# Bucketed attention and two mixtures of experts on one core: buckets as twelve bit columns with their sums in the scores' tiles, and the integer tile of the weights' words in PSUM

## The chip, the core and the metric

One core of a Trainium2 chip runs the whole program in one launch. The metric is the device time of one execution in microseconds. The engines are TensorE (PE, with its weight loads as PEld), VectorE (DVE), ScalarE (ACT), GpSimd (POOL) and SyncE (SP), which issues nearly all DMAs. TensorE's clock has two levels, 1.2 and 2.4 GHz; the profile gives the granted clock of a stretch as a share of the higher one.

## What is computed

The reference, cut to the part that the change touches:

```
def _attn_ref(q, k, v, proj):             # q, k, v: 2 x 8 x 768 x 64, proj: 64 x 6
    q_bits = (np.einsum('bhsd,dk->bhsk', q, proj) > 0)
    k_bits = (np.einsum('bhsd,dk->bhsk', k, proj) > 0)
    q_bucket = np.sum(q_bits * powers, axis=-1)       # powers = 2 ** arange(6)
    k_bucket = np.sum(k_bits * powers, axis=-1)
    mask = q_bucket[:, :, :, None] == k_bucket[:, :, None, :]
    scores = np.where(mask, scale * np.matmul(q, k.transpose(0, 1, 3, 2)), -1000000000.0)
    scores = scores - np.max(scores, axis=-1, keepdims=True)
    attn = np.exp(scores)
    attn = attn / (np.sum(attn, axis=-1, keepdims=True) + 1e-09)
    return np.matmul(attn, v)
def _moe_ref(x, w_in, w_out):             # 1536 x 512, 512 x 2048, 2048 x 512
    h = x @ w_in
    return (h * (1.0 / (1.0 + np.exp(-1.702 * h)))) @ w_out
```

A query sees only the keys whose six sign bits are the same as its own. A dense layer follows (its two weight matrices arrive as 64-bit floats), and then a layer of eight experts with a noisy top-2 choice, which the change doesn't touch.

## The kernel before

**Tiling.** Attention is cut into 96 steps g: for each of 2 batches, 3 chunks of 256 queries, 4 pairs of heads, 2 heads and 2 halves of 128 queries, one score tile of 128 queries by 768 keys. A score is a sum of two products of 128 rows each (`qk`, line 256): one over the high and low parts of q and k, one over their high parts in 64 rows and the bucket in another 64. Numbers are kept to nearly fp32 by splitting each into two f16 parts, so that a product is three f16 products.

**A unit of q or k.** There are 24 units of q (two heads, 256 queries) and 16 of k (one head, 768 keys). `stack_hi` and `stack_lo` split the rows into tiles sa and sb (qsa, qsb, or ks), on VectorE, GpSimd (line 147, the residual) and ScalarE, and a DMA transposes sa. `buckets` multiplies the transposed rows by proj on TensorE, into a PSUM tile pb of which there is one; ScalarE copies it to pc (line 186). `one_hot` then compares (line 191), multiplies by powers of two (193), sums (196) and compares the bucket with the numbers 0 to 63 (202 or 205), which gives 64 one-hot columns; `stack_end` scales them on ScalarE in 28 of the 40 units (212) and a DMA transposes sb (213). A pair of one-hot rows adds nothing to the score where the buckets agree and takes a large number away where they don't.

**A step.** `rowmax` (line 268) is a custom VectorE op that reads the score tile from PSUM, negates it into tile e and keeps the smallest of -score/8 as a column mx; `expo` (277) takes exponentials on ScalarE with mx as bias; splits, transposes by DMA (`et<-er`) and the product with v follow. Score tiles are two, 128 x 1024 fp32 each, of which 768 columns are used.

**The weights of the dense layer** come in 32 blocks of 128 x 512 words. `w_bits` makes a 32-bit float of a 64-bit one with three integer ops on VectorE (lines 430, 433, 436) through a tile wf in SBUF, of which there is one; `w_split` makes the two f16 parts on ScalarE and GpSimd. All 32 blocks are spread over the steps up to g = 24.

**The order.** Functions are hung on steps by tables in `PARAM` (KA, QA, W, PV and others), and a scheduler that plans with its own durations sets the order on each engine up to step 100; after that the order is the program's. Engines run their lists in order. The dense layer of a chunk runs between the score products of the next one, and the experts follow the attention.

Of the kernel before, what the change touches and what calls it, by code (L numbers as in the profile page):

```python
# [36 lines left out]
NBITS = 6  # L37
NB = 2 ** NBITS
BIG = 65504.0
TOP = 3.0e38  # L40
# [18 lines left out]


@with_exitstack
def fused(ctx: ExitStack, tc: tile.TileContext, q, k, v, proj, w_in, w_out, w_gate, w_noise, noise,
# [13 lines left out]

    iota_i = consts.tile([128, NB], F16)
    nc.gpsimd.iota(iota_i, pattern=[[1, NB]], base=0, channel_multiplier=0,
                   allow_small_or_imprecise_dtypes=True)
# [52 lines left out]
    def stack_hi(nm, b, u):  # L132
# [9 lines left out]
        rows[nm, b, u] = sa, sb  # L142
        h0 = 0 if nm == "q" else 64
# [3 lines left out]
        nc.gpsimd.tensor_tensor(x.rearrange(FL), x.rearrange(FL), hi, op=OP.subtract)  # L147
# [40 lines left out]
    def one_hot(nm, b, u):  # L188
        pc = bks.pop((nm, b, u))
        nb, bb = pc.shape[1], pc[:, :, :NBITS]  # L190
        nc.vector.tensor_tensor(bb, bb, pc[:, :, NBITS:], op=OP.is_gt)
        yield
        nc.vector.tensor_tensor(bb, bb, pow2[:, None, :].to_broadcast([128, nb, NBITS]), op=OP.mult)
        yield
        bk = att.tile([128, nb], F32, name="bk", bufs=2)
        nc.vector.tensor_reduce(bk, bb, axis=AX.X, op=OP.add)
        yield
        oh = rows[nm, b, u][0][:, :, :, 64:].rearrange(FL)
        if PARAM["OE"](nm, b) != "D":
            eng = nc.gpsimd if PARAM["OE"](nm, b) == "P" else nc.vector  # L200
            for i in range(nb):
                eng.tensor_scalar(oh[:, i], iota_i, bk[:, i:i + 1], -BIG if nm == "k" else BIG,
                                        op0=OP.not_equal if nm == "k" else OP.is_equal, op1=OP.mult)
            return
        nc.vector.tensor_tensor(oh, iota_i[:, None, :].to_broadcast([128, nb, NB]),
                                bk[:, :, None].to_broadcast([128, nb, NB]), op=OP.is_equal)

    def stack_end(nm, b, u):
        sb, xt = rows.pop((nm, b, u))
        oh = sb[:, :, :, 64:].rearrange(FL)  # L210
        if PARAM["OE"](nm, b) == "D":
            nc.scalar.activation(oh, oh, AF.Identity, scale=BIG, bias=-BIG if nm == "k" else 0.0)
        nc.sync.dma_start_transpose(xt[:, 1].rearrange("p h c t -> p (h c) t"), sb.rearrange("p h c d -> p (h c d)"))
# [21 lines left out]
    def v_lo(b, u):  # L235
# [3 lines left out]
        nc.gpsimd.tensor_tensor(vt[:, :, 1, sl], x, vt[:, :, 0, sl], op=OP.subtract)  # L239
# [9 lines left out]
    def qk(g):  # L249
# [12 lines left out]
    def rowmax(g):  # L262
# [5 lines left out]
        nc.vector.tensor_tensor_reduce(e32, st[g]["ps"][:, :S], zero.to_broadcast([128, S]), -0.125, TOP,  # L268
                                       op0=OP.add, op1=OP.min, accum_out=mx[:, 1:2])

    def expo(g):
# [5 lines left out]
        nc.scalar.activation(e32, e32, AF.Exp, scale=-1.0, bias=st[g]["mx"][:, 1:2],  # L277
# [110 lines left out]
    def pv_out(b, cc, hp):  # L388
# [11 lines left out]
        nc.gpsimd.tensor_tensor(xt[:, hp, 1, :], xn, xt[:, hp, 0, :], op=OP.subtract)  # L400
# [830 lines left out]
```

## Time and profile before

| | |
|---|---|
| runs, us | 813.56, 815.48, 811.27 (median 813.56) |
| profiled execution, us | 812.06, of which the span is 810.4 |
| granted clock of TensorE, mean | 0.963 |
| busy: PE, DVE, ACT, POOL | 703.6, 539.5, 446.6, 271.1 us |
| instructions: PE, DVE, ACT, POOL | 5408, 1368, 866, 305 |

The table is read for a first picture only: TensorE is busy 87% of the span, VectorE 67%, but an average over the run mixes stages with different limits, so the rows below are cut by stretches of time. A group of instructions is named by its line of the program, the engine, the operation and the tiles that it writes and reads (`out<-in`). "Idle before" is the time in which the engine waited ahead of these instructions, with what ended most of the waiting.

### The profile page before, as it was taken

The page shows a single profiled execution, that of the slowest core. Times are in us where ns is not written, and L with a number is a line of the kernel's source. Part 1 is how long each engine was busy: PE and PEld are TensorE (multiplying, and loading weights), DVE is VectorE, ACT ScalarE, POOL GpSimd, SP SyncE. Part 2 cuts the span into 40 slices and gives each one's busy share as a digit, 9 for nine tenths or more (in the row PEclk, how much of TensorE's full clock was granted, in tenths as well). Part 3 has the DMA queues.
Part 4 walks back from the last instruction along what each step waited for, and adds up shares of the span by engine and source line. Part 5 has one row for each costly group of instructions (what it writes and reads, how often), then busy time and mean ns, then how long its engine had stood idle before and what let it go on. Part 6 is the DMA issues. An engine that isn't in the chain of part 4 may idle for free.

```text
span 810.4 us, 14910 instructions
## 1 busy us (share of the span) xinstructions
PE 703.6 (87%) x5408; PEld 435.3 (54%) x5409; DVE 539.5 (67%) x1368; ACT 446.6 (55%) x866; POOL 271.1 (33%) x305
## 2 busy tenths in 40 slices
PE   1576578988888898789899999998999999999995
PEld 1343346646754585458457667465555545555452
DVE  8998689997896879659878815682735436354220
ACT  3678768775775686467657614452634425344220
POOL 6444646651444045314212223331130211302113
PEclk9889779999999998999999999999999999999998
DMA  8999678999999898996798772837968577584213
GB/s 220 213 258 224 161 181 192 243 289 237 172 164 196 157 196 178 213 187 105 124 175 132 115 253 38 203 150 192 259 133 252 123 194 232 77 255 89 26 18 44
DMA packets 266943, 139.20 MB, mean 172 GB/s; under 512 B 224177, under 2 KB 242673, under 8 KB 266865
## 3 DMA queue, kind: packets, MB, share of 16 engines
q1 hardware_dynamic: 260848, 125.04, 68.6%
q0 software_dynamic: 6016, 13.16, 9.1%
q8 instruction: 43, 0.70, 0.4%
q14 instruction: 36, 0.29, 0.1%
HBM read 61.48 MB, written 23.20 MB: 105 GB/s over the span
## 4 chain that ended last, share of the span: by engine, by line
PE 41%; DVE 5%; DMA 4%; ACT 2%; issue 1%; POOL 1%; POOLq 0%; ACTq 0%; DVEq 0%
PE ph L837 15%; PE py L868 14%; PE px L473 6%; PE h L462 3%; DMA et<-er 2%; PE py L862 1%; PE pv L370 1%; PE s L256 1%; DVE th L492 1%; DVE er L325 1%; DMA xg<-slots 1%; DMA slots<-xr,si 0%; ACT er L316 0%; ACT gt L506 0%; DMA qt<-qsb 0%
## 5 line engine op out<-in xcount | busy, mean ns | idle before, releaser
L462 PE MATMUL h<-xt,wi 128*128 128x256 f16 x1152 | 142.2, 279 | 6.5 <-DVE th L492 3.2
L837 PE MATMUL ph<-xg,ew 128*128 128x400 f16 (+2 forms) x864 | 133.9, 317 | 4.3 <-DMA xg<-slots 3.7
L473 PE MATMUL px<-wo,gt 128*128 128x512 f16 x576 | 131.1, 379 | 0.1
L777 DVE SCALAR_TENSOR_TENSOR ew<-w,ew 128x1024 f16<-128x1024 f32 x64 | 77.8, 1226 | 78.6 <-ACT ew L776 78.6
L462 PEld LDWEIGHTS <-wi 128*128 128x128 f16 x1152 | 113.8, 100 | 29.5 <-issue 9.4
L868 PE MATMUL py<-ew,ht 128*128 128x512 f16 x576 | 125.8, 379 | 0.0
L885 POOL DMA_INDIRECT out_dram<-yo,ti x32 | 53.8, 1683 | 203.5 <-ACT yo L878 197.7
L256 PE MATMUL s<-kt,qt 128*128 128x512 f16 (+1 forms) x384 | 87.2, 350 | 37.0 <-DVE mx L268 31.3
L837 PEld LDWEIGHTS <-ew 128*128 128x128 f16 x864 | 81.9, 99 | 54.2 <-issue 6.2
L277 ACT ACTIVATE e<-e,mx 128x768 f32<-128x768 f32 x96 | 89.4, 931 | 29.3 <-DVE mx L268 23.4
L507 POOL TENSOR_TENSOR gt<-th,gt 128x512 f16<-128x512 f32 x48 | 60.7, 1266 | 123.9 <-ACT gt L506 123.5
L268 DVE CUSTOM_DVE_ANT_0 e<-s,zero 128x768 f32<-128x768 f32 x96 | 90.7, 949 | 7.0 <-PE pt L295 2.9
L868 PEld LDWEIGHTS <-ht 128*128 128x128 f16 x576 | 56.2, 98 | 67.0
L325 DVE SCALAR_TENSOR_TENSOR er<-e,mx,er 128x768 f16<-128x768 f32 x68 | 71.1, 1049 | 27.4 <-ACT er L316 26.8
L473 PEld LDWEIGHTS <-gt 128*128 128x128 f16 x576 | 54.9, 98 | 62.3 <-issue 0.6
L316 ACT ACTIVATE er<-e,mx 128x768 f16<-128x768 f32 x68 | 63.2, 930 | 41.8 <-DMA et<-er 27.5
L256 PEld LDWEIGHTS <-qt 128*128 128x128 f16 x384 | 36.6, 102 | 66.4 <-issue 41.0
L878 ACT ACTIVATE yo<-py,wv 128x512 f32<-128x512 f32 x24 | 16.5, 688 | 94.1 <-PE py L868 57.4
L847 ACT ACTIVATE ht<-ph 128x400 f16<-128x400 f32 (+2 forms) x72 | 33.5, 466 | 62.0 <-PE ph L837 61.3
L776 ACT ACTIVATE ew<-w 128x1024 f16<-128x1024 f32 x64 | 66.2, 1048 | 0.1
L848 DVE SCALAR_TENSOR_TENSOR ht<-ph,ht 128x400 f16<-128x400 f32 (+2 forms) x72 | 37.5, 524 | 39.3 <-ACT ht L847 39.1
L370 PE MATMUL pv<-et,vt 128*64 128x256 f16 x720 | 50.5, 281 | 9.3 <-DMA et<-er 9.3
(234 smaller groups left out, 942.5 us busy)
## 6 DMA issues: line engine op xcount, KB each, us to landing
w<-in_moe_w_dram SPq DMA_DIRECT2D x64, 512.0 KB, 5.8
wraw<-in_moe_w_in_dram SPq DMA_DIRECT2D x16, 512.0 KB, 4.6
wraw<-in_moe_w_out_dram SPq DMA_DIRECT2D x16, 512.0 KB, 4.3
slots<-blank SPq DMA_DIRECT2D x6, 1032.0 KB, 6.4
v<-in_v_dram SPq DMA_DIRECT2D x24, 192.0 KB, 4.5
out_dram<-zeros SPq DMA_DIRECT2D x13, 256.0 KB, 3.3
k<-in_k_dram SPq DMA_DIRECT2D x16, 192.0 KB, 3.9
q<-in_q_dram SPq DMA_DIRECT2D x24, 128.0 KB, 3.3
```

What stands on the lines that cost most here:

```text
L256: nc.tensor.matmul(ps[:, n0 * 128:n1 * 128], qt[:, s, h, t, :], kt[:, s, h, n0:n1, :].rearrange("p c t -> p (c t)"), start=(s == 0), stop= ...
L268: nc.vector.tensor_tensor_reduce(e32, st[g]["ps"][:, :S], zero.to_broadcast([128, S]), -0.125, TOP, op0=OP.add, op1=OP.min, accum_out=mx[: ...
L277: nc.scalar.activation(e32, e32, AF.Exp, scale=-1.0, bias=st[g]["mx"][:, 1:2], accum_out=sms[b, cc, hp][:, 2 * h + t:2 * h + t + 1] if g < ...
L316: nc.scalar.activation(er[:, 0], st[g]["e"], AF.Copy, scale=r)
L325: nc.vector.scalar_tensor_tensor(er[:, 1], d["e"], d["mx"][:, 3:4], er[:, 0], op0=OP.mult, op1=OP.subtract)
L462: nc.tensor.matmul(ph[:, a, :], wi[ws][:, d, f0:f0 + 128], xt[:, d, xs, :], start=(d == 0 and ws == 0 and xs == 0), stop=(d == HP - 1 and ...
L473: nc.tensor.matmul(px, gts[ci, f // 2][:, gs, f % 2, t * 128:t * 128 + 128], wo[ws][:, f, :], start=(f == 0 and gs == 0 and ws == 0), stop ...
L507: nc.gpsimd.tensor_tensor(gt[:, 1], th, gt[:, 0], op=OP.subtract)
L776: nc.scalar.activation(hi, x, AF.Copy, scale=SW1 if j == 0 else SW2)
L777: nc.vector.scalar_tensor_tensor(lo, x, SW1 if j == 0 else SW2, hi, op0=OP.mult, op1=OP.subtract)
L837: nc.tensor.matmul(ph[:, :c1 - c0], w[:, ws, d * FE + f * 128:d * FE + f * 128 + 128], xg[e, p][:, xs * HP + d, :], start=(d == 0 and ws = ...
L868: nc.tensor.matmul(py, ht[:, f, hs, t * 128:t * 128 + 128], w[:, ws, f * DM:(f + 1) * DM], start=(i == 0), stop=(i == n - 1))
```

## The change

A bucket becomes twelve columns in place of 64: six that hold a scaled 1 where the bit is set, and six where it isn't (for k the other way round), so that their product takes a large number away for each bit that differs. VectorE makes them with two comparisons; the remaining columns of sb are set to zero by a GpSimd memset for each unit (line 138 of the changed program). The bucket sums go to unused columns of the score tile that is two steps ahead, and no longer to pb. The second score product reads 76 rows. The row maximum is a plain tensor_scalar that keeps the largest score and leaves the sign, and a ScalarE op of one column makes the bias of the exponential. The integer tile of `w_bits` lies in PSUM, in the buffer that pb had. The flags XS, GS, XN and the lower-case letters of WS choose what the kernel did already; `w_rest` only drops a name.

```diff
+KB = 64 + 2 * NBITS
+FAR = 2.0 ** 31
...
+        nc.gpsimd.memset(sb[:, :, :, KB:].rearrange(FL), 0.0)
...
-        pb = psr.tile([128, nh * n, 2 * NBITS], F32, name="pb", bufs=1)
+        w0 = nh * n * 2 * NBITS
+        s = st.get(now[0] + 2)
+        if s is None:
+            s = {"ps": pss.tile([128, 1024], F32, name="s")}
+        a0 = s.get("end", S)
+        s["end"] = a0 + w0
+        assert s["end"] <= 1024
+        pb = s["ps"][:, a0:a0 + w0].rearrange("p (m k) -> p m k", k=2 * NBITS)
...
-        nb, bb = pc.shape[1], pc[:, :, :NBITS]
-        nc.vector.tensor_tensor(bb, bb, pc[:, :, NBITS:], op=OP.is_gt)
-        yield
-        nc.vector.tensor_tensor(bb, bb, pow2[:, None, :].to_broadcast([128, nb, NBITS]), op=OP.mult)
-        yield
-        bk = att.tile([128, nb], F32, name="bk", bufs=2)
-        nc.vector.tensor_reduce(bk, bb, axis=AX.X, op=OP.add)
-        yield
-        oh = rows[nm, b, u][0][:, :, :, 64:].rearrange(FL)
-        if PARAM["OE"](nm, b) != "D":
-            eng = nc.gpsimd if PARAM["OE"](nm, b) == "P" else nc.vector
-            for i in range(nb):
-                eng.tensor_scalar(oh[:, i], iota_i, bk[:, i:i + 1], -BIG if nm == "k" else BIG,
-                                        op0=OP.not_equal if nm == "k" else OP.is_equal, op1=OP.mult)
-            return
-        nc.vector.tensor_tensor(oh, iota_i[:, None, :].to_broadcast([128, nb, NB]),
-                                bk[:, :, None].to_broadcast([128, nb, NB]), op=OP.is_equal)
+        oh = rows[nm, b, u][0][:, :, :, 64:64 + 2 * NBITS].rearrange(FL)
+        for j in range(2):
+            nc.vector.tensor_tensor(oh[:, :, j * NBITS:(j + 1) * NBITS], pc[:, :, :NBITS], pc[:, :, NBITS:],
+                                    op=OP.is_le if j == (nm == "q") else OP.is_gt)
+            yield
...
-        oh = sb[:, :, :, 64:].rearrange(FL)
-        if PARAM["OE"](nm, b) == "D":
-            nc.scalar.activation(oh, oh, AF.Identity, scale=BIG, bias=-BIG if nm == "k" else 0.0)
+        oh = sb[:, :, :, 64:64 + 2 * NBITS].rearrange(FL)
+        nc.scalar.activation(oh, oh, AF.Copy, scale=-BIG if nm == "k" else BIG)
...
+            kr = KB if s else 128
             for n0, n1 in ((0, 4), (4, 6)):
-                nc.tensor.matmul(ps[:, n0 * 128:n1 * 128], qt[:, s, h, t, :],
-                                 kt[:, s, h, n0:n1, :].rearrange("p c t -> p (c t)"),
+                nc.tensor.matmul(ps[:, n0 * 128:n1 * 128], qt[:kr, s, h, t, :],
+                                 kt[:kr, s, h, n0:n1, :].rearrange("p c t -> p (c t)"),
                                  start=(s == 0), stop=(s == 1))
...
-        nc.vector.tensor_tensor_reduce(e32, st[g]["ps"][:, :S], zero.to_broadcast([128, S]), -0.125, TOP,
-                                       op0=OP.add, op1=OP.min, accum_out=mx[:, 1:2])
+        nc.vector.tensor_scalar(e32, st[g]["ps"][:, :S], -FAR, -TOP, op0=OP.max, op1=OP.max, accum_out=mx[:, 0:1])
...
-        nc.scalar.activation(e32, e32, AF.Exp, scale=-1.0, bias=st[g]["mx"][:, 1:2],
+        nc.scalar.activation(st[g]["mx"][:, 1:2], st[g]["mx"][:, 0:1], AF.Copy, scale=-0.125)
+        nc.scalar.activation(e32, e32, AF.Exp, scale=0.125, bias=st[g]["mx"][:, 1:2],
...
-            f = moe.tile([128, 512], F32, name="wf", bufs=1)
-            fi = f.bitcast(I32)
+            fi = psr.tile([128, 512], I32, name="pfi", tag="pb", bufs=1)
```

The scheduler plans anew, so the order moves on all engines, though by the step g hardly any. Three places:

VectorE at the first two score tiles. L191, L193, L196 and L205 are the bucket code of a unit, L268 the row maximum and the read of its accumulator, L430 the first op on the words. Before:

```order
L191 TENSOR_TENSOR pc<-pc 128x6x6
L268 ISA e_351,mx<-s,zero 128x768
L268 ISA mx 128x1
L268 ISA e_395,mx<-s,zero 128x768
L268 ISA mx 128x1
L193 TENSOR_TENSOR pc<-pc,pow_92 128x6x6
L191 TENSOR_TENSOR pc<-pc 128x4x6
L196 TENSOR_REDUCE bk<-pc 128x6
L193 TENSOR_TENSOR pc<-pc,pow_92 128x4x6
L430 TENSOR_SCALAR wf<-wraw 128x512
L205 TENSOR_TENSOR ks<-iota_i,bk 128x6x64
L196 TENSOR_REDUCE bk<-pc 128x4
```

After, where L196 is a comparison, L261 the row maximum and L423, L426 and L429 the ops on the words:

```order
L196 TENSOR_TENSOR ks<-pc 128x6x6 x2
L261 TENSOR_SCALAR e_332,mx<-s 128x768
L196 TENSOR_TENSOR ks<-pc 128x6x6 x2
L261 TENSOR_SCALAR e_374,mx<-s 128x768
L423 TENSOR_SCALAR pfi<-wraw 128x512
L426 SCALAR_TENSOR_TENSOR pfi<-wraw,pfi 128x512
L429 SCALAR_TENSOR_TENSOR wraw<-wraw,pfi 128x512
L196 TENSOR_TENSOR qsb<-pc 128x4x6 x2
```

A unit's four rows have become one row of two ops, which stands ahead of the row maximum in place of around it.

GpSimd at the start, ahead of the first residual of k (L147). Before:

```order
L528 IOTA tok 128x12
L532 MEMSET blank 128x8
L535 MEMSET blank_120 128x8
L718 MEMSET spacer 1x1
L518 AFFINE_SELECT before<-before 128x128
L533 IOTA blank 128x1
L537 IOTA blank_120 32x1 x4
L718 MEMSET spacer 1x1
L147 TENSOR_TENSOR k_136<-k_136,ks 128x384
```

After, where L144 is that residual and L138 the new memset:

```order
L540 MEMSET blank_109 128x8
L138 MEMSET ks 128x6x52
L138 MEMSET qsb 128x4x52
L138 MEMSET ks 128x6x52 x3
L138 MEMSET qsb 128x4x52
L723 MEMSET spacer 1x1
L538 IOTA blank 128x1
L542 IOTA blank_109 32x1 x4
L144 TENSOR_TENSOR k_125<-k_125,ks 128x384
```

Six memsets now stand ahead of the first residual.

TensorE where a unit of k has its bucket products (L181 and L182) near a score tile (L256). Before:

```order
L181 LDWEIGHTS kt
L181 MATMUL pb<-pk,kt 128x12
L256 LDWEIGHTS qt
L256 MATMUL s<-kt,qt 128x512
L256 LDWEIGHTS qt
L256 MATMUL s<-kt,qt 128x256
L256 LDWEIGHTS qt
L256 MATMUL s<-kt,qt 128x512
L256 LDWEIGHTS qt
L256 MATMUL s<-kt,qt 128x256
L182 LDWEIGHTS kt
L182 MATMUL pb<-pk,kt 128x6
```

After (L185 and L186, and L249):

```order
L249 LDWEIGHTS qt
L249 MATMUL s<-kt,qt 128x512
L249 LDWEIGHTS qt
L249 MATMUL s<-kt,qt 128x256
L249 LDWEIGHTS qt
L249 MATMUL s<-kt,qt 128x512
L249 LDWEIGHTS qt
L249 MATMUL s<-kt,qt 128x256
L185 LDWEIGHTS kt
L185 MATMUL s<-pk,kt 128x12
L186 LDWEIGHTS kt
L186 MATMUL s<-pk,kt 128x6
```

The bucket products stood wherever the scheduler had room, and now follow the score products of their tile and write the same tile s.

## Rows read from the trace of the kernel before

**Rows 1.** Stretches, busy us (xcount): PE, PEld, DVE, ACT, POOL; PEclk, DMA share, GB/s

```profile
0.00:160.00 160.00, 101.99 (x820) 68.02 (x822) 142.82 (x320) 113.28 (x248) 88.35 (x119) 0.88 0.90 209
160.00:240.00 80.00, 68.60 (x593) 45.27 (x592) 71.74 (x186) 56.26 (x117) 33.03 (x31) 1.00 1.05 224
240.00:440.00 200.00, 179.34 (x1516) 118.73 (x1516) 152.99 (x445) 128.30 (x258) 62.56 (x59) 0.97 0.92 166
440.00:812.00 372.00, 353.63 (x2487) 203.29 (x2482) 171.91 (x420) 148.78 (x247) 87.15 (x98) 0.99 0.60 147
```

**Rows 2.** Waits of TensorE, 0 to 160 us: total us, times, longest

```profile
PE s L256 <- DVE mx L268: 20.4, 12, 3.6
PE pb L181 <- DMA kt<-ks: 14.6, 3, 9.0
PE pb L181 <- DMA qt<-qsa: 7.4, 3, 3.7
```

**Rows 3.** Waits of VectorE, 0 to 160 us

```profile
DVE wf L430 <- DMA wraw<-in_moe_w_out_dram: 3.3, 2, 2.5
```

**Rows 4.** Waits of TensorE, 160 to 440 us

```profile
PE s L256 <- DVE mx L268: 10.9, 12, 1.8
PE pv L370 <- DMA et<-er: 9.3, 6, 2.9
...
PE pb L181 <- DMA qt<-qsa: 1.6, 1, 1.6
```

**Rows 5.** Busy us by stretch on tile pc: PE, DVE, ACT; PEclk, DMA, GB/s

```profile
0.00:160.00 160.00, 0.00 (x0) 14.68 (x51) 3.60 (x17) 0.88 0.90 209
160.00:240.00 80.00, 0.00 (x0) 6.40 (x21) 1.42 (x7) 1.00 1.05 224
240.00:440.00 200.00, 0.00 (x0) 12.21 (x48) 3.25 (x16) 0.97 0.92 166
```

**Rows 6.** Busy us by stretch on tile iota_i: DVE, POOL; PEclk, DMA, GB/s

```profile
0.00:160.00 160.00, 11.54 (x17) 0.19 (x1) 0.88 0.90 209
160.00:240.00 80.00, 5.10 (x11) 0.00 (x0) 1.00 1.05 224
240.00:440.00 200.00, 17.57 (x49) 0.00 (x0) 0.97 0.92 166
```

**Rows 7.** Groups by shape, VectorE: busy us, mean ns; idle before

```profile
L191 DVE TENSOR_TENSOR pc<-pc 128x24 f32<-128x24 f32 x24 | 7.3, 305 | 0.2 <-ACT pc L186 0.2
```

**Rows 8.** Busy us by stretch on tile wf: DVE; PEclk, DMA, GB/s

```profile
0.00:160.00 160.00, 61.64 (x85) 0.88 0.90 209
160.00:240.00 80.00, 9.25 (x12) 1.00 1.05 224
```

**Rows 9.** Instructions on tile wf: ns min/median/max, first and last start us

```profile
L430 DVE TENSOR_SCALAR wf<-wraw x32: 411/421/1400, 7.3 to 176.8; 128x512 int32<-128x512 int32 x32
L433 DVE SCALAR_TENSOR_TENSOR wf<-wraw,wf x32: 677/692/2151, 7.7 to 178.1; 128x512 int32<-128x512 int32 x32
```

**Rows 10.** Line 492, same columns

```profile
L492 DVE SCALAR_TENSOR_TENSOR th<-th,h x48: 652/680/690, 124.5 to 505.0; 128x512 f32<-128x512 f32 x48
```

**Rows 11.** Groups by shape, VectorE, the row maximum

```profile
L268 DVE CUSTOM_DVE_ANT_0 e<-s,zero 128x768 f32<-128x768 f32 x96 | 90.7, 949 | 7.0 <-PE pt L295 2.9 <-PE s L256 2.2
```

**Rows 12.** Groups by shape, VectorE, line 848 (reads PSUM)

```profile
L848 DVE SCALAR_TENSOR_TENSOR ht<-ph,ht 128x400 f16<-128x400 f32 x56 | 32.0, 571 | 30.3 <-ACT ht L847 30.2
...
L848 DVE SCALAR_TENSOR_TENSOR ht<-ph,ht 128x256 f16<-128x256 f32 x8 | 3.3, 417 | 0.5 <-ACT ht L847 0.5
```

**Rows 13.** Groups by shape, ScalarE

```profile
L683 ACT ACTIVATE d<-d 128x2 f32<-128x2 f32 x5 | 1.0, 194 | 3.5 <-DVE d L680 3.5
```

**Rows 14.** Timeline of GpSimd from the start: start us, us

```profile
1.10 0.20 POOL L81 MEMSET ident<- 128x128 f16 x1
...
1.66 0.09 POOL L90 MEMSET pow<- 128x1 f32 x1
...
3.88 0.92 POOL L147 TENSOR_TENSOR k<-k,ks 128x384 f32<-128x384 f32 x1 [0.42 <-DVE ks L146]
```

More of the change, by code (lines that the diff above doesn't have):

```diff
@@ L37 @@
 NBITS = 6
-NB = 2 ** NBITS
 BIG = 65504.0
+KB = 64 + 2 * NBITS
+FAR = 2.0 ** 31
 TOP = 3.0e38
@@ L75, in fused @@
     pss = pss_ctx.enter_context(tc.tile_pool(name="pss", bufs=2, space=bass.MemoryType.PSUM))
-    iota_i = consts.tile([128, NB], F16)
-    nc.gpsimd.iota(iota_i, pattern=[[1, NB]], base=0, channel_multiplier=0,
-                   allow_small_or_imprecise_dtypes=True)
     ident = consts.tile([128, 128], F16)
@@ L83, in fused @@
                             channel_multiplier=1)
-    zero = consts.tile([128, 1], F32)
-    nc.vector.memset(zero, 0.0)
     ident32 = consts.tile([128, 128], F32)
     nc.vector.tensor_copy(ident32, ident)
-    pow2 = consts.tile([128, NBITS], F32)
-    for i in range(NBITS):
-        nc.gpsimd.memset(pow2[:, i:i + 1], float(2 ** i))
     pr = {nm: consts.tile([128, 3, NBITS], F16, name=f"p{nm}") for nm in "qk"}
@@ L146, in stack_hi @@
         eng.tensor_scalar(hi, x.rearrange(FL), GX, GX, op0=OP.add, op1=OP.subtract)
-        nc.gpsimd.tensor_tensor(x.rearrange(FL), x.rearrange(FL), hi, op=OP.subtract)
+        eng = nc.gpsimd if PARAM["XS"](nm, b) == "P" else nc.vector
+        eng.tensor_tensor(x.rearrange(FL), x.rearrange(FL), hi, op=OP.subtract)
         yield
@@ L238, in v_lo @@
         sl = slice(h * 64, h * 64 + 64)
-        nc.gpsimd.tensor_tensor(vt[:, :, 1, sl], x, vt[:, :, 0, sl], op=OP.subtract)
+        eng = nc.gpsimd if PARAM["XS"]("v", b) == "P" else nc.vector
+        eng.tensor_tensor(vt[:, :, 1, sl], x, vt[:, :, 0, sl], op=OP.subtract)
     st, ets, xts, pos, sms = {}, {}, {}, {}, {}
@@ L399, in pv_out @@
         nc.scalar.activation(xt[:, hp, 0, :], xn, AF.Copy)
-        nc.gpsimd.tensor_tensor(xt[:, hp, 1, :], xn, xt[:, hp, 0, :], op=OP.subtract)
+        eng = nc.gpsimd if PARAM["XN"] == "P" else nc.vector
+        eng.tensor_tensor(xt[:, hp, 1, :], xn, xt[:, hp, 0, :], op=OP.subtract)
     wi = [wts.tile([128, HP, FF], F16, name=f"wi{i}", tag="w") for i in range(2)]
@@ L441, in w_split, with w_rest @@
         hi, lo, src, scale = wblocks[i]
-        f = wraw.pop(i)
-        if PARAM["WS"](i) == "P":
-            nc.gpsimd.tensor_scalar(f, f, scale, 1.0, op0=OP.mult, op1=OP.mult)
-        else:
-            nc.scalar.activation(f, f, AF.Copy, scale=scale)
-        nc.scalar.activation(hi, f, AF.Copy)
-        nc.gpsimd.tensor_tensor(lo, f, hi, op=OP.subtract)
+        f, m = wraw[i], PARAM["WS"](i)
+        if m == "P":
+            nc.gpsimd.tensor_scalar(hi, f, scale, 1.0, op0=OP.mult, op1=OP.mult)
+        elif m == "A":
+            nc.scalar.activation(hi, f, AF.Copy, scale=scale)
+        else:
+            if m == "p":
+                nc.gpsimd.tensor_scalar(f, f, scale, 1.0, op0=OP.mult, op1=OP.mult)
+            else:
+                nc.scalar.activation(f, f, AF.Copy, scale=scale)
+            nc.scalar.activation(hi, f, AF.Copy)
+            nc.gpsimd.tensor_tensor(lo, f, hi, op=OP.subtract)
+    def w_rest(i):
+        hi, lo, src, scale = wblocks[i]
+        f = wraw.pop(i)
+        if PARAM["WS"](i) in "AP":
+            nc.vector.scalar_tensor_tensor(lo, f, scale, hi, op0=OP.mult, op1=OP.subtract)
     gts, mst = {}, {}
@@ L506, in moe_split @@
             nc.scalar.activation(gt[:, 0], th, AF.Copy)
-            nc.gpsimd.tensor_tensor(gt[:, 1], th, gt[:, 0], op=OP.subtract)
+            eng = nc.gpsimd if PARAM["GS"](ci, i) == "P" else nc.vector
+            eng.tensor_tensor(gt[:, 1], th, gt[:, 0], op=OP.subtract)
             if (ci, i) in clear:
@@ L972, in fused @@
                 soon(g + 1, w_split, wl)
+                at(g + 1, w_rest, wl)
                 wl += 1
@@ L1027, in fused @@
     g_lo = min(todo)
+    now = [0]
     for g in range(g_lo, G1 + 1):
+        now[0] = g
         if g == max(PARAM["GM"], g_lo):
```

1 line of the change is left out of this document (added).

## Prediction

> **What bounds the kernel now.** I read the stretches of the whole run first [rows 1]. From 440 us on, TensorE is busy 353.6 of the last 370 us and VectorE 171.9: next to nothing that the change touches lies there, so whatever it saves or costs before 440 us arrives at the end one for one. Before that the kernel has three different limits. In 0 to 160 us VectorE is busy 142.8 of 160 us, TensorE 102.0, ScalarE 113.3, GpSimd 88.4. In 160 to 240 us VectorE (71.7 of 80) and TensorE (68.6) are both near full and the DMA share is 1.05. In 240 to 440 us TensorE leads with 179.3 of 200, VectorE has fallen to 153.0.
>
> Then the waits. In 0 to 160 us TensorE's largest wait is for the row maxima that set a score tile free (20.4 us); after it come the transposes of k, of whose 14.6 us 9.0 are the very first load, and those of q with 7.4 [rows 2]. VectorE's own longest wait there is 3.3 us in all [rows 3]: it is the engine that others wait for. In 160 to 440 us TensorE still waits 10.9 us for row maxima, and 9.3 for the transposes of the exponentials [rows 4]. So a VectorE microsecond is worth most of a microsecond before 160 us, perhaps half until 240, and little after.
>
> **The bucket code on VectorE.** Before, a unit (24 of q, 16 of k) costs a comparison, a product and a sum on tile pc, and then the one-hot columns from iota_i. By stretch, pc and iota_i together take 14.7 + 11.5 = 26.2 us, 6.4 + 5.1 = 11.5 us and 12.2 + 17.6 = 29.8 us [rows 5, 6]. ScalarE's copies into pc count the units: 17, 7 and 16 [rows 5]. After, a unit is two comparisons like line 191, of 0.305 us on average [rows 7]: 34 x 0.305 = 10.4, 14 x 0.305 = 4.3 and 32 x 0.305 = 9.8 us, so -15.8, -7.2 and -20.0 us. The output is now f16 in rows 128 columns apart, a form that no row of this op has. I bound one comparison by half and by twice that mean, 0.15 and 0.6: 12 us more saved or 24 given back over the 80.
>
> **The weights' words.** The three ops on wf take 61.6 and 9.3 us, 2.2 us for each of 32 blocks [rows 8]. The first two have medians of 421 and 692 ns but worst cases of 1400 and 2151: they are held up [rows 9]. Line 492, which has one operand in PSUM, is 652 to 690 and never held [rows 10]. With the tile in PSUM I price the three as three such ops, 3 x 0.68 = 2.04 us: 28.3 blocks (85 ops) in the first stretch 57.8 us (-3.8), 4 in the second 8.2 (-1.1). Bounds: the first op at 0.41 and the others at 0.65 gives 1.71 (-16 us in all); the first at 0.68 and the hold-ups unchanged gives 2.47 (+8 us). I choose the value between since line 492 has the same shape.
>
> Two rules bear on it, and they pull apart. The trace has line 430 at 0.42 us for 512 columns [rows 9], while ops that read PSUM pay 1.07 ns a column (below). The Trainium skill, "VectorE: DVE Perf Modes", section "Why PSUM operands drop a tier", says that an operand in PSUM leaves an fp32 op at one element a cycle, which speaks against the change: by it alone a block that nothing disturbs goes from 1.80 to 2.04 us, 7.7 us lost over 32. Against that stand the hold-ups of [rows 9] beside none in [rows 10]: the Trainium skill, "SBUF — State Buffer", section "Who interferes with whom", lets an op with two SBUF inputs wait for a GpSimd op that reads SBUF, and one with a single SBUF input not; the trace agrees, and by it the hold-ups go.
>
> **The row maximum.** Before, 949 ns, 96 times [rows 11]. After, a tensor_scalar with an accumulator on the same 128x768 tile in PSUM. No row shows one. Ops that read PSUM take 417 and 571 ns for 256 and 400 columns [rows 12]: (571 - 417) / 144 = 1.07 ns a column and 0.14 fixed, so 0.965 us for 768, 0.016 more than now, 1.5 us over all 96, which I put at 0.5 in each stretch. Were it to run at line 430's pace, 768 x 0.421 / 512 = 0.63 us, the 96 would save 31 us; I keep that for the low end.
>
> **ScalarE.** A multiplication of 128x1 now stands between row maximum and exponential. Its like is 194 ns [rows 13]: 96 x 0.194 = 18.6 us, most of it before 440 us where ScalarE is busy 298 of 440 [rows 1]. So it hides under the other engines in throughput; to each tile it adds 0.2 us of latency, which two score tiles in flight cover. If that cover fails, it costs its 18 us. The factor on the bucket columns becomes shorter; I count nothing for it.
>
> **GpSimd.** 40 memsets of 208 or 312 columns are new. A memset of 128 columns takes 0.20 us and one of one column 0.09 [rows 14], 0.87 ns a column, so 0.27 and 0.36: 24 x 0.27 + 16 x 0.36 = 12 us, on an engine with 72 us free before 160. Six of them (2.0 us) stand ahead of the first subtraction, and iota_i and pow2 (about 0.4 us) go. GpSimd had 0.42 us idle before that subtraction at 3.88 us [rows 14], so it starts some 1.2 us later, and with it the first transpose, for which everything waits: +1.2 us. Later memsets wait for the transpose that frees their buffer, with the residuals of q, k and the weights queued behind; the op that followed before waited for the same buffer, so I cost it at nothing.
>
> **Scores' tiles, TensorE.** The second score product reads 76 rows in place of 128; its columns, 512 and 256, are the same, so I give it no time, between a small gain and a small loss. The transposes keep their size. The bucket products lose the wait for their own single buffer, but the row maximum of their tile now waits for them (rival c).
>
> **The sum.** VectorE: -19.1, -7.8, -19.5 us in the three stretches. Of the first I return two thirds, 12.7, because 17 of its 160 us are idle already and the DMA share is 0.90; less 1.2 for the start, 11.5. Of the second half, 3.9, since TensorE has only 11.4 us free there. Of the third a fifth, 3.9, since row maxima are only a part of what TensorE waits for. Together -19.3 us: from the profiled execution's 812.06 us (span 810.4) to 793; the median of the runs is 1.5 us above the profiled one, which I leave inside the range.
>
> **Rivals.** (a) The saving returns whole: 19.1 - 1.2 before 160 us, 7.8 in the second stretch and half of TensorE's 20.7 idle us in the third, -36 us, 776; a cheaper row maximum goes lower. For it: VectorE waits for almost nothing in [rows 3]. Against: TensorE and DMA are near full from 160 us on.
> (b) It is hidden: transfers set the pace. The DMA share is 0.94 on average up to 440 us. If that is the limit, VectorE only idles more and the late start remains: 813. Against: the stretch 160 to 240 us carries 1.05.
> (c) Slower: the sums in the scores' tiles tie two things together. In the built program 23 of the 96 row maxima wait for the last bucket product in their tile and no longer just for the scores. That product waits for a transpose; VectorE works in order, so everything behind the row maximum waits as well. After the first load, TensorE waited for a q transpose four times, 7.4 + 1.6 = 9.0 us, 2.25 each [rows 2, 4]. If every one of the 23 is hit, 52 us are lost: 793 + 52 = 845. It decides from 19.3 / 2.25 = 9 of them on. Against it: TensorE runs the products well ahead of the maximum, and in 160 to 440 us only one such wait exists.
> (d) The word ops do not get shorter (the first goes to 0.68, the hold-ups stay): 8 in place of -5 us on VectorE, two thirds of 11 us of it in time before 160, 800. This is inside my forecast.
>
> **How the numbers follow.** Forecast with (d), 785 to 804: 0.52. (a), 771 to 785: 0.16. (b), 804 to 816: 0.13, of which 0.03 below 808. (c): 0.15. The remaining 0.04 is a gain beyond (a). The range 771 to 815 leaves out (c) and that rest. A measurement of this kernel tells about 0.5%, 4 us, from no change. Faster by more than that: 0.52 + 0.16 + 0.03 + 0.04 = 0.75; within it 0.10; slower 0.15.
>
> **What would show it.** The two comparisons of a unit at about 0.3 us each, the three word ops with worst times close to their medians, the row maximum at 0.95 to 0.97. VectorE's busy time near 493 us in place of 539.5, and the work that now stands at 160 us at about 148. TensorE's wait for the row maximum shrinking in the first stretch. It is wrong if that wait stays and the row maximum itself waits for bucket products (c), if the gaps before 160 us turn into waits for DMA (b), or if the row maximum is not as long as its columns say.

## Result and profile after

The changed kernel takes 803.5 us (median), the kernel before 812.4 in the same set of runs: ratio 0.9887, 95% interval 0.9865 to 0.991. It is faster, by 8.9 us. The forecast was 793.0, a gain of 19.3 us; the measured gain is just under half of it. The profiled execution took 806.2 us with a span of 804.5, against 812.1 and 810.4. One of the ten runs took 933.7 us at a granted clock of 0.752: the median counts it, the ratio doesn't. What is said below of single stretches and steps comes from one profiled execution of each kernel, and these lie up to 4 us off their medians.

The page's first lines after, span and busy time by engine:

```profile
span 804.5 us, 14892 instructions
PE 706.8 (88%) x5408; PEld 435.2 (54%) x5409; DVE 502.6 (62%) x1251; ACT 458.3 (57%) x974; POOL 270.2 (34%) x338
```

The stretches after (columns as in [rows 1]):

```profile
0.00:160.00 160.00, 108.48 (x845) 70.20 (x847) 133.26 (x295) 119.18 (x284) 88.86 (x134) 0.88 0.92 227
160.00:240.00 80.00, 71.40 (x630) 48.47 (x629) 62.74 (x175) 58.45 (x136) 34.77 (x38) 0.96 1.03 208
240.00:440.00 200.00, 179.52 (x1521) 118.28 (x1520) 140.63 (x378) 136.94 (x316) 66.46 (x71) 0.97 0.89 164
440.00:804.00 364.00, 347.36 (x2418) 198.28 (x2415) 165.99 (x408) 143.69 (x240) 80.13 (x96) 0.99 0.59 147
```

VectorE's busy time fell from 539.5 to 502.6 us. Against [rows 1], VectorE lost 9.6, 9.0 and 12.4 us in the first three stretches; TensorE gained 6.5 and 2.8 in the first two and nothing in the third. ScalarE rose by 5.9, 2.2 and 8.6 us.

Single lines after, instructions with ns min/median/max, first and last start: the two comparisons (196), the words (423, 426, 429), the row maximum (261), ScalarE's new multiplication (269), GpSimd's memsets (138):

```profile
L196 DVE TENSOR_TENSOR qsb<-pc x48: 142/176/1191, 16.3 to 428.9; 128x24 f16<-128x24 f32 x48
L196 DVE TENSOR_TENSOR ks<-pc x32: 177/189/992, 15.9 to 286.2; 128x36 f16<-128x36 f32 x32
L423 DVE TENSOR_SCALAR pfi<-wraw x32: 675/692/741, 7.7 to 168.6; 128x512 int32<-128x512 int32 x32
L426 DVE SCALAR_TENSOR_TENSOR pfi<-wraw,pfi x32: 677/690/712, 8.6 to 170.5; 128x512 int32<-128x512 int32 x32
L429 DVE SCALAR_TENSOR_TENSOR wraw<-wraw,pfi x32: 669/682/721, 10.0 to 172.7; 128x512 int32<-128x512 int32 x32
L261 DVE TENSOR_SCALAR_CACHE_REDUCE e<-s x96: 927/950/968, 24.0 to 453.3; 128x768 f32<-128x768 f32 x96
L269 ACT ACTIVATE mx<-mx x96: 180/202/211, 25.0 to 454.3; 128x1 f32<-128x1 f32 x96
L138 POOL MEMSET qsb<- x24: 262/272/283, 2.6 to 386.0; 128x208 f16 x24
L138 POOL MEMSET ks<- x16: 348/358/571, 2.3 to 268.8; 128x312 f16 x16
```

The comparisons again as groups by shape (busy us, mean ns | idle before):

```profile
L196 DVE TENSOR_TENSOR qsb<-pc 128x24 f16<-128x24 f32 x48 | 10.8, 264 | 0.2 <-ACT pc L190 0.2
L196 DVE TENSOR_TENSOR ks<-pc 128x36 f16<-128x36 f32 x32 | 6.7, 249 | 1.6 <-ACT pc L190 1.6
```

Most prices of the sum came in as put: words 2.06 us a block (forecast 2.04), row maximum 0.95 (0.965), multiplication 0.20 (0.194), memsets 0.27 and 0.36. The comparisons were cheaper, 17.5 us of busy time for all 80 where 24.4 were put. The first of the word operations went from a median of 421 ns to 692 and the hold-ups of [rows 9] are gone. So no operation was much dearer than put, and the question is where 10 us of gain went.

TensorE's waits in 0 to 160 us after (total us, times, longest), which answer [rows 2]:

```profile
PE s L249 <- DVE e L261: 16.9, 13, 4.4
PE s L185 <- DMA kt<-ks: 14.9, 2, 14.3
PE s L249 <- DMA qt<-qsb: 7.5, 2, 4.5
PE h L466 <- ACT xt L392: 5.9, 1, 5.9
```

VectorE's waits in 0 to 160 us after ([rows 3] had 3.3 us as the longest sum):

```profile
DVE pfi L423 <- DMA wraw<-in_moe_w_in_dram: 12.9, 8, 5.8
DVE qsb L142 <- DMA qt<-qsb: 3.4, 2, 2.0
DVE er L316 <- ACT er L309: 3.1, 1, 3.1
```

and in 160 to 440 us:

```profile
DVE er L318 <- ACT er L309: 37.2, 38, 5.1
DVE mx L274 <- ACT e L270: 18.2, 21, 4.5
```

VectorE now waits: before 160 us for the loads of the words (13.8 us with those of the other matrix, 5.0 before the change), from 160 to 440 us for ScalarE's exponential and er (55.4 us, 36.3 before). I measured progress by the start of the row maxima, one per step (96 of them; the 30th and the last below count from 0):

| kernel | row maximum 30 starts | steps 30 to 95 | row maximum 95 starts | rest of the span |
|---|---|---|---|---|
| before | 167.5 | 291.2 | 458.7 | 351.7 |
| after | 160.3 | 293.0 | 453.3 | 351.2 |

The whole gain of the profiled run arises before step 30 (7.2 us), and 1.8 of it are given back in steps 30 to 95, where VectorE works some 20 us less. The rest passes one for one, as put.

### The profile page after: what moved, and what is told of

Its sections match the earlier page's. It is cut to its first block, busy times and chain, and to the rows that moved or that the text cites. A ratio compares the mean times of both kernels' runs of the same rounds, so it can differ in the third digit from the quotient of the medians.

```text
span 804.5 us, 14892 instructions
## 1 busy us (share of the span) xinstructions
PE 706.8 (88%) x5408; PEld 435.2 (54%) x5409; DVE 502.6 (62%) x1251; ACT 458.3 (57%) x974; POOL 270.2 (34%) x338
## 5 line engine op out<-in xcount | busy, mean ns | idle before, releaser
L466 PE MATMUL h<-xt,wi 128*128 128x256 f16 x1152 | 139.8, 277 | 11.4 <-ACT xt L392 5.9
L249 PE MATMUL s<-kt,qt 128*128 128x512 f16 (+3 forms) x384 | 91.4, 362 | 37.8 <-DVE e L261 27.7
L890 POOL DMA_INDIRECT out_dram<-yo,ti x32 | 49.9, 1560 | 207.6 <-ACT yo L883 199.5
L261 DVE TENSOR_SCALAR_CACHE_REDUCE e<-s 128x768 f32<-128x768 f32 x96 | 90.7, 949 | 2.5 <-PE s L249 0.9
L512 POOL TENSOR_TENSOR gt<-th,gt 128x512 f16<-128x512 f32 x48 | 56.5, 1178 | 98.4 <-ACT gt L510 97.4
L249 PEld LDWEIGHTS <-qt 76*128 76x128 f16 (+1 forms) x384 | 36.1, 104 | 68.9 <-issue 32.9
L883 ACT ACTIVATE yo<-py,wv 128x512 f32<-128x512 f32 x24 | 16.5, 688 | 94.1 <-PE py L873 57.4
```

The lines of the kernel that those rows point to most:

```text
L249: nc.tensor.matmul(ps[:, n0 * 128:n1 * 128], qt[:kr, s, h, t, :], kt[:kr, s, h, n0:n1, :].rearrange("p c t -> p (c t)"), start=(s == 0), s ...
L261: nc.vector.tensor_scalar(e32, st[g]["ps"][:, :S], -FAR, -TOP, op0=OP.max, op1=OP.max, accum_out=mx[:, 0:1])
L466: nc.tensor.matmul(ph[:, a, :], wi[ws][:, d, f0:f0 + 128], xt[:, d, xs, :], start=(d == 0 and ws == 0 and xs == 0), stop=(d == HP - 1 and ...
```

## Experiments

All times are medians, ratios are to the kernel before on the same chip with 95% intervals. "Row" means the order in which an engine's instructions stand.

### One part undone at a time

Row maximum of the kernel before, which delivers its result negated and scaled, so that ScalarE has no 128x1 operation:

```
-        nc.vector.tensor_scalar(e32, st[g]["ps"][:, :S], -FAR, -TOP, op0=OP.max, op1=OP.max, accum_out=mx[:, 0:1])
+        nc.vector.tensor_tensor_reduce(e32, st[g]["ps"][:, :S], zero.to_broadcast([128, S]), -0.125, TOP,
+                                       op0=OP.add, op1=OP.min, accum_out=mx[:, 1:2])
...
-        nc.scalar.activation(st[g]["mx"][:, 1:2], st[g]["mx"][:, 0:1], AF.Copy, scale=-0.125)
-        nc.scalar.activation(e32, e32, AF.Exp, scale=0.125, bias=st[g]["mx"][:, 1:2],
+        nc.scalar.activation(e32, e32, AF.Exp, scale=-1.0, bias=st[g]["mx"][:, 1:2],
```

> The changed kernel with one part undone: the row maximum and the negated scores of the kernel before, so that ScalarE has no 128x1 multiplication between row maximum and exponential (96 of 197 ns, 18.9 us). VectorE's row maximum is 947 to 949 ns in both forms. Theory S (the added ScalarE operation lies on the chain row maximum, exponential, er, that paces the steps; VectorE waits for er 37.2 us in 160 to 440 us where it waited 25.2 before): half to all of the 66 x 0.2 = 13 us of 160 to 440 us come back, 790 to 797 us, and VectorE's wait for er falls below 30 us. Theory T (transfers set the pace from 40 us on, DMA share 1.05 in 40 to 80 and 1.06 in 160 to 200 us): 802 to 804. Theory G (GpSimd, held in order by its new memsets, sets the pace): 802 to 804.

797.2 us, ratio 0.9826 (0.9789 to 0.9862): 6.3 us less, the upper edge of what S allowed. But VectorE's wait for er stayed at 35.0 us, which S had put below 30: that part of S fell.

The opposite on the kernel before, the operation added:

```
+        nc.scalar.activation(st[g]["mx"][:, 0:1], st[g]["mx"][:, 1:2], AF.Copy)
         nc.scalar.activation(e32, e32, AF.Exp, scale=-1.0, bias=st[g]["mx"][:, 0:1],
```

> The kernel before with one thing added: ScalarE copies the 128x1 row maximum to another column ahead of each exponential, 96 operations of about 0.2 us, and the exponential waits for it. Theory S: half to all of 19 us are lost, 822 to 831 us. Theories T and G, under which ScalarE has room: 812 to 815.

813.1 us, ratio 1.0013 (0.9994 to 1.0033): there it is free, against S. At this point the 6.3 us above could as well have come from another row.

The memset behind the residual:

```
-        nc.gpsimd.memset(sb[:, :, :, KB:].rearrange(FL), 0.0)
...
         eng.tensor_tensor(x.rearrange(FL), x.rearrange(FL), hi, op=OP.subtract)
+        nc.gpsimd.memset(sb[:, :, :, KB:].rearrange(FL), 0.0)
```

> The changed kernel with the memset of the unused columns put behind the residual of q or k on GpSimd in place of ahead of the rounding. GpSimd stands idle 59.6 us ahead of the 40 memsets, most of it waiting for the transposes that free the buffers (47.8 and 11.8 us). Theory G: what stands behind the memsets in GpSimd's row comes earlier, the first residual at about 3.9 us in place of 4.85, the wait of TensorE for xt (5.9 us) shrinks, 796 to 800 us. Theories S and T: 802 to 805, the wait only moves to the residual, which needs the same buffer.

798.9 us, ratio 0.9848 (0.9814 to 0.9882), as G had it, though the first residual starts at 4.39 us and not at 3.9. Both together:

> The changed kernel with the row maximum of the kernel before (no 128x1 operation on ScalarE) and the memsets behind the residuals, the two steps that gave 6.3 and 4.6 us when taken alone. If they are two costs beside each other: 803.5 - 6.3 - 4.6 = 792 to 794 us. If both only remove the same waiting before 160 us (row maximum 30 at 155.4 and 156.7 us in place of 160.3): 796 to 799. In either case steps 30 to 95 take 286 to 292 us, as in all kernels so far, if VectorE and ScalarE aren't the pace there.

799.7 us, 0.9839 (0.9812 to 0.9867): no more than either alone. Two costs that lie beside each other would have given 793.

The words' tile in SBUF again:

```
-            fi = psr.tile([128, 512], I32, name="pfi", tag="pb", bufs=1)
+            f = moe.tile([128, 512], F32, name="wf", bufs=1)
+            fi = f.bitcast(I32)
```

> The changed kernel with one part undone: the integer tile of the weights' words lies in SBUF again. The three operations go from 691, 691, 683 ns back to about 510, 810, 900 ns, 2.2 us a block, +4.8 us on VectorE. By the prediction's rule of two thirds before 160 us: 803.5 + 3 = 806 to 808. If VectorE isn't the pace there (T): 803 to 805. If most of the gain comes from this part: 810 to 812.

820.0 us, ratio 1.0103 (1.0061 to 1.0145): beyond all three expectations, and slower than the kernel before. 16.5 us for 8 us of VectorE work can hardly be the operations alone.

### The sums in the scores' tiles

On top of the last one, the bucket sums in their own tile, as before:

```
-        pb = s["ps"][:, a0:a0 + w0].rearrange("p (m k) -> p m k", k=2 * NBITS)
+        pb = psr.tile([128, nh * n, 2 * NBITS], F32, name="pb", bufs=1)
```

> Like the changed kernel with the words' tile in SBUF (820.0 us, slower than before by 1%), and in addition the bucket sums in a tile of their own again, so that no row maximum waits for a bucket product. Rival of the prediction (sums in the scores' tiles tie row maxima to transposes): that is what made 820, and the time goes to 806 to 812. If what made it slow is VectorE being held up by GpSimd's operations (words 74.2 us in place of 66.1, other operations held too): 816 to 822.

808.3 us, ratio 0.995 (0.993 to 0.9969), 11.7 us less. The kernel before with only the words' tile in PSUM, which forces the sums into the scores' tiles:

> The kernel before with the words' tile in PSUM alone; the sums of the buckets, which lay there, go to the scores' tiles as in the change; 64 one-hot columns, the row maximum and everything else as before. If the words' part carries the whole gain and the 12 columns bring nothing: 798 to 804 us. If the parts add up by VectorE's time (words -4.8 of some 55 us): 808 to 812. If the tie to the scores' tiles costs what the parts gain: 814 or more.

817.1 us, 1.0057 (1.0038 to 1.0077): slower than before by 4.7 us. Both runs speak for rival (c), though each has a row of its own. So I tried the changed kernel with an own tile for the sums, the two score tiles back to back in three banks:

```
-        ps = pss.tile([128, 1024], F32, name="s")
+        ps = sall[:, g % 2 * S:g % 2 * S + S]
...
-            for n0, n1 in ((0, 4), (4, 6)):
+            for n0, n1 in ((0, 4), (4, 6)) if g % 2 == 0 else ((0, 2), (2, 6)):
...
+        pb = pss.tile([128, nh * n, 2 * NBITS], F32, name="pbk", bufs=1)
```

> The changed kernel with the bucket sums in a tile of their own again, beside the words' tile in PSUM: the two score tiles of 768 columns lie back to back in three banks, which leaves one for the sums (every other step's scores are split 256 and 512 columns in place of 512 and 256). No row maximum waits for a bucket product. The own tile was worth 820.0 - 808.3 = 11.7 us with the words in SBUF. If the tie costs the changed kernel the same: 790 to 795 us. If the words in PSUM and the own tile save the same waiting: 799 to 805.

843.1 us, 1.0371 (1.0337 to 1.0406). And without the 128x1 operations:

> The same with the row maximum of the kernel before, so without the 128x1 operation on ScalarE (6.3 us alone). If own tile and row maximum add up: 784 to 790 us. If one waiting hides the other, as with the memsets (803.5, 797.2, 798.9, together 799.7): 792 to 799. The prediction had 793 for the change and 776 if all of VectorE's saving came back.

830.7 us, 1.0223 (1.0188 to 1.0258). Neither expectation held: steps 30 to 95 take 314 and 311 us in place of 293. Two waits of the first of these: VectorE's for scores (total us, times, longest), and TensorE's for et, which stands behind the second bar of the line (busy us, mean ns | idle before):

```profile
DVE e L255 <- PE s L243: 9.8, 13, 1.2
```

```profile
L357 PE MATMUL pv<-et,vt 128*64 128x256 f16 x720 | 53.1, 288 | 21.4 <-DMA et<-er 21.4
```

In the changed kernel the row maxima wait 0.9 us for scores in all, and TensorE 9.9 us for et. The row maximum still takes 949 ns. Why the engines wait more here is not settled; these two kernels also got rows of their own.

### Holding the rows

Each edit changes what the scheduler believes, and so the row on every engine: with the words' tile in SBUF at least 249 of VectorE's 802 instructions and 216 of ScalarE's 669 up to step 100 change places. To part edit and row, a table now gives each engine's row up to step 100. It adds no wait, and in the traces of the runs below every engine's operations stand in the row that was meant, but for those that the edit itself changes:

```
+def pin_order(tc, nc):
...
+        for p, q in zip(seq, seq[1:]):
+            tc.add_manual_dep(rows[e][q], rows[e][p].name, mybir.DependencyInfo(
+                mybir.DependencyClass.NoSync, mybir.DependencyReason.DATA), reason="order")
```

Words in SBUF, row of the changed kernel:

> Words' tile in SBUF, and each engine's instructions before step 100 kept in the row of the changed kernel (a table gives the row, the waits are unchanged). When the scheduler chose a row for it, the same program took 820.0 us. Theory W (the operations on the words, held up in SBUF, cost the time by themselves): 816 to 822 also in this row. Theory R (most of the 16.5 us came from the other row): 804 to 809, VectorE's 5 to 8 us of longer word operations being returned at two thirds before 160 us.

810.0 us, ratio 0.9963 (0.9941 to 0.9985). The changed kernel itself in the row of the 820.0 us kernel:

> The changed kernel with nothing but its row changed: each engine's instructions before step 100 stand in the row that the scheduler chose with the words' tile in SBUF (820.0 us). Theory W: 802 to 806. Theory R: 812 to 818.

812.0 us, 0.9995 (0.9973 to 1.0016).

| | row of the changed kernel | row chosen with the words in SBUF |
|---|---|---|
| words' tile in PSUM | 803.5 | 812.0 |
| words' tile in SBUF | 810.0 | 820.0 |

The tile is worth 6.5 to 8.0 us in either row, the row 8.5 to 10.0 with either tile: R and W each hold a part, and the two add up. The word operations of the 810.0 us kernel (groups by shape, VectorE: busy us, mean ns; idle before):

```profile
L453 DVE SCALAR_TENSOR_TENSOR wf<-wraw,wf 128x512 int32<-128x512 int32 x32 | 30.1, 941 | 0.2
L456 DVE SCALAR_TENSOR_TENSOR wraw<-wraw,wf 128x512 int32<-128x512 int32 x32 | 28.5, 891 | 0.7
L450 DVE TENSOR_SCALAR wf<-wraw 128x512 int32<-128x512 int32 x32 | 16.2, 505 | 8.3 <-DMA wraw<-in_moe_w_in_dram 7.3 <-DMA wraw<-in_moe_w_out_dram 0.9
```

They sum to 74.8 us, against 66.1 in PSUM: 8.7 us of VectorE time, of which 6.5 reach the end, three quarters. Row maximum 30 starts at 167.1 in place of 160.3, so all of it arises before step 30. The trace also shows what stands beside the hold-ups: all 28 word operations that took over 1.1 times their median ran beside a GpSimd operation, and none of the 39 that ran alone took so long. In the changed kernel 62 of the 96 run beside one, and the longest takes 741 ns. The third operation with the tile in SBUF (ns min/median/max):

```profile
L456 DVE SCALAR_TENSOR_TENSOR wraw<-wraw,wf x32: 672/693/1676, 9.9 to 179.5; 128x512 int32<-128x512 int32 x32
```

The granted clock before 160 us is 0.83 in this run and in the 812.0 us one, 0.88 in the changed kernel. How much of the lost time is TensorE's lower clock is not parted; the clock alone doesn't decide it, since the 797.2 us kernel had 0.85 there and reached row maximum 30 at 155.4 us.

The same for ScalarE's multiplication. Without it, in the row of the changed kernel:

> Row maximum of the kernel before, no 128x1 operation on ScalarE, all other instructions kept in the row of the changed kernel; with the scheduler's own row the same program took 797.2 us. Theory S (the 96 operations of 0.2 us cost time on the chain): 796 to 799. Theory R (the row made the 6.3 us): 801 to 804.

797.4 us, ratio 0.9811 (0.979 to 0.9832): 6.1 us less with nothing else moved. With it, in the row chosen without it:

> The changed kernel with nothing but its row changed: each engine's instructions before step 100 stand in the row that the scheduler chose without the 128x1 operations (797.2 us), these again just ahead of their exponentials. Theory S: 802 to 805. Theory R: 796 to 799.

802.1 us, 0.988 (0.9859 to 0.9902). Here the row is worth 1.4 us at most and the operation 4.9 to 6.1: S holds, R falls. In the profiled runs 2.0 us come before step 30 and 6.0 in steps 30 to 95 (287.0 us in place of 293.0), and 0.9 are lost behind the attention; with the other row these steps take 296.9 with the operation and 290.0 without. Which wait carries the cost is not shown. In 160 to 440 us of the 797.4 us kernel TensorE waits 4.6 us for row maxima in place of 10.9, and VectorE 51.3 for ScalarE in place of 55.4:

```profile
PE s L277 <- DVE mx L289: 4.6, 6, 1.8
DVE er L346 <- ACT er L337: 37.9, 43, 2.3
DVE mx L302 <- ACT e L298: 13.4, 18, 4.2
```

But the kernel with the moved memsets, next, has the operation and shows only 6.0 us of the first of these waits.

The memsets behind the residuals, all rows but GpSimd's held:

> The changed kernel with the 40 memsets placed right behind the residual of their unit in GpSimd's row; the rows of all other engines stay those of the changed kernel. With the scheduler's own rows the same edit took 798.9 us. Theory G (GpSimd held by the memsets, 59.6 us idle ahead of them, and a first residual 0.97 us later than before): 798 to 800. Theory R (the row made the 4.6 us): 802.5 to 805.

802.4 us, 0.9886 (0.9861 to 0.991): the same as the changed kernel. G falls; the 4.6 us of the free version came from its row. This run also stands for the changed kernel with its row given by a table, which was not run by itself.

### What sets the pace of steps 30 to 95

One of the three products of the dense layer's first matmul left out:

```
-                    for ws, xs in ((0, 0), (0, 1), (1, 0)):
+                    for ws, xs in ((0, 0), (1, 0)):
```

> The changed kernel with one of the three products of the dense layer's first matmul left out (the low half of the tokens by the high half of the weights), 384 of 1152 matmuls of 277 ns, 46.6 us of TensorE's busy time, of which some 28 us lie in 160 to 440 us. Nothing else changes. Theory P (TensorE, busy 251 of these 280 us, sets the pace of steps 30 to 95, so that VectorE's savings there return nothing): these steps take 262 to 275 us in place of 293, the time is 765 to 780. Theory T (transfers set it, DMA share 0.93): the steps stay at 285 to 293 and only what lies after 440 us returns, 788 to 796.

795.6 us, 0.9784 (0.9753 to 0.9816), steps 30 to 95 in 289.9 us. TensorE was busy 236.1 us of 160 to 440 in place of 250.9, at a granted clock of 0.93 in place of 0.97, and the steps became 3 us shorter: TensorE's work alone does not set their pace, as far as a run in a row of its own shows it (some 450 of VectorE's 1251 instructions stand elsewhere). Of the 6.7 us between the profiled runs, 2.1 come before row maximum 95 and 4.6 behind it.

The writes of zeros moved behind the attention (`O0=98, OS=1`), and done twice:

> The changed kernel with the 14 writes of zeros to the output (3.3 MB, from 225 to 342 us in the trace) moved behind the attention, from step 98 on, where the DMA share is 0.58. Steps 30 to 95 took 288 to 293 us in every kernel so far, also with 28 us less work for TensorE. Theory T (transfers set that pace, DMA share 0.93): 3.3 MB are 9 us at the fastest 370 GB/s of the rows, 18 at the mean of 180; these steps take 275 to 284 us, the time is 788 to 797. Theory C (the chain from row maximum through exponential, er and its transpose, with two buffers of er, sets it): they stay at 286 to 293, the time is 800 to 805.

> The changed kernel with each of the 14 writes of zeros done twice at its place: 3.3 MB more, the counterpart to moving them. Theory T: steps 30 to 95 take 9 to 18 us longer, 812 to 821 us. Theory C: 803 to 807.

799.7 us (0.9854, 0.9808 to 0.9901) and 809.9 us (0.9975, 0.9949 to 1.0). Steps 30 to 95 took 284.0 and 296.8 us around 293.0. Their stretches 160 to 440 us, the moved one and the doubled one:

```profile
160.00:440.00 280.00, 256.25 (x2247) 172.30 (x2247) 209.85 (x570) 204.77 (x471) 102.66 (x111) 0.98 0.89 171
```

```profile
160.00:440.00 280.00, 248.45 (x2111) 163.46 (x2110) 196.48 (x544) 192.02 (x445) 98.28 (x107) 0.96 0.94 187
```

3.3 MB change these steps by 4 to 9 us, where 9 to 18 were expected of transfers alone, and neither time lies in a range that T or C gave; so transfers seem to set a part of the pace. The rows here are nearly those of the changed kernel (some 50 and 140 of VectorE's 1251 instructions stand elsewhere). Last, both of what had helped, in the row of the changed kernel:

> The changed kernel in its own row, with two things taken from it: the 128x1 operations on ScalarE (row maximum of the kernel before; 797.4 us in this row) and the 14 writes of zeros, which move behind the attention (799.7 alone, with the scheduler's row). If the chain through ScalarE and the transfers are two costs beside each other in steps 30 to 95: 793 to 795 us, the forecast's number. If in those steps only one of them ends last at a time: 796 to 798.

796.1 us, 0.98 (0.9766 to 0.9834); steps 30 to 95 in 284.7 us. Against 797.4 without the moved writes the difference lies within the intervals. This speaks for the second reading, that in these steps one of the two ends last at a time; the interval, some 5 us wide, doesn't rule out the first. It is the fastest kernel that I found that computes everything, together with the 797.2 and 797.4 us ones.

## Why the prediction was half right

**VectorE as the limit before 160 us: right in the main.** Words in the same row give 6.5 us of time for 8.7 us of work, 0.75, where I took two thirds, with the reserve on the clock above. The hold-ups of [rows 9] did vanish: the worst word operation is 741 ns after, 1676 with the tile in SBUF in the same row, and each of the held ones ran beside GpSimd. For the second and third operation, with two inputs in SBUF, this is what the Trainium skill, "SBUF — State Buffer", section "Who interferes with whom", lets one expect. The first has a single input in SBUF and was held up all the same, to 1400 ns in [rows 9]: the prediction left out that the section exempts such an operation only outside the modes that use both ports. The rule of "VectorE: DVE Perf Modes", section "Why PSUM operands drop a tier", also held (421 to 692 ns) but was the smaller of the two: 66.1 us against 74.8.

**The step that failed: ScalarE.** The prediction wrote that the multiplication "hides under the other engines in throughput" and that two score tiles in flight cover its 0.2 us of latency. With the rows held it costs 4.9 to 6.1 us, a quarter to a third of its 18.9. The prediction had the price if the cover fails, 18 us, and gave it no case. That it costs time is shown; by which way is argued. In [rows 1] ScalarE is busy 113 of 160 us, which reads as room; but in 160 to 440 us VectorE's instructions wait for ScalarE's, 37.2 + 18.2 us after, and the next row maximum stands behind them in VectorE's row. On the kernel before the same operation was free (813.1 us, its rows not held). This would fit a cover that was there as long as VectorE had more to do and that the change took away; no run with held rows shows it.

**The size of VectorE's saving: a fifth too large.** The durations of all VectorE operations (busy times of all its groups by line) sum to 611.9 us before and 565.0 after, -46.9. That this is so near the forecast (-46.4) is chance: the bucket code gave 50 us where 43 were put, since the comparisons were cheaper, the words 4.8 as put, and VectorE's other operations, which the change leaves alone, took some 8 us longer. And busy time fell by 36.9 only: short operations overlap their neighbours, and with 117 fewer instructions 10 us of overlap go, some 85 ns each. The forecast "VectorE near 493" was 502.6; the seven others that keep VectorE's part of the change whole had 498 to 504. The Trainium skill, "Perfetto Trace Analysis", section "Optimizing Scalar/DVE Operations", says that about half of a profiled instruction's latency overlaps the next one; this trace agrees in direction and not in size, since the 10 us are a fifth of the 50 us by which the removed operations were longer. A fifth off the 20.5 us that I returned is 4.1 us: with the 6.1 us of ScalarE this comes to 10.2 of the 10.4 that are missing. The 4.1 are a sum that fits, not a number that an experiment shows; the rows that the scheduler chose for before and after may hold some of it, since rows alone moved the same program by up to 10 us.

**The returned shares, by steps.** Before step 30, about the first stretch, the prediction returned 11.5 us; 7.2 came, and 9.2 without the multiplication in the same row. In steps 30 to 95 it returned 3.9 + 3.9 us; without the multiplication 4.2 came (291.2 to 287.0), with it none. That VectorE is no limit in these steps was right; that TensorE is, as "TensorE has only 11.4 us free" supposed, was not borne out: 15 us less of its work gave 3.

**The late start: right in its cause, no matter in time.** The first residual starts at 4.85 us in place of 3.88 [rows 14], 0.97 late where 1.2 was forecast. The first bucket product starts at 14.3 in place of 9.0, much later than that, for a cause that stays open; yet the first row maximum starts at 24.0 us in place of 26.0. With the memsets behind the residuals it starts at 24.1 and the time is the same.

**Memsets "at nothing": not contradicted.** Their place costs nothing in the held row (802.4); no run leaves them out.

**Rivals.** (a) needed all of it back; no. (b), transfers, is true in part: VectorE's largest wait before 160 us is now for the words' loads, 13.8 us in place of 5.0. This is one of the signs of being wrong that the prediction named, and the 8.8 us more are nearly the 9.6 by which VectorE's busy time fell there. And 3.3 MB are worth 4 to 6 us of time. (c), the tie: in the changed kernel no row maximum waited for a bucket product, the wait for scores is 0.9 us in all. Two runs speak for a cost of 11.7 us or so when the sums go to the scores' tiles, but with rows of their own, so edit and row were not parted; the own tile in the changed kernel made it slower. What the tie costs stays open. (d) was wrong: the word operations got shorter, 66.1 us in all against 70.9 in [rows 8] and 74.8 in the same row.

## What to carry to other kernels

An operation of 0.2 us on an engine with room need not be free when it stands between two engines that wait for each other in order: look at who waits for that engine, not at its busy share, and ask whether the change removes the work that covered it. Where a scheduler orders the program, an edit also buys another order; here that was worth up to 10 us, more than the whole gain, so undo a part with the order held before you believe what undoing it shows. Count the removed work of short operations in busy time, not as the sum of their durations.

## What the runs showed of the hardware

- An integer tensor_scalar of 512 columns takes 421 ns between SBUF tiles and 692 ns into PSUM, but the three word operations together are 8.7 us shorter over 32 blocks with the intermediate in PSUM, since none is held up: with it in SBUF 28 of 96 took over 1.1 times their median, each beside a GpSimd operation.
- A tensor_scalar with an accumulator from PSUM takes the same 949 ns for 768 columns as the operation that it replaced.
- The comparisons, on 24 or 36 columns, have a median of 176 and 189 ns and a worst of 1191 and 992: 8 of the 80 took over 300 ns, each beside a GpSimd operation. The medians alone would be 48 x 0.176 + 32 x 0.189 = 14.5 us, the busy time of the 80 is 17.5 and their durations sum to 20.7.
- With two score tiles that share a bank the row maximum also took 949 ns.
